# Attention output projection: one f32 product in column tiles, or three products of rounded parts in full tiles

## The chip, the cores and the metric

The kernel runs on one core of a Trainium2 chip. A core has five engines with queues of their own: TensorE (PE, matmuls), VectorE (DVE), ScalarE (ACT), GpSimd (POOL) and SyncE (SP, which here issues all DMA transfers). The metric is the device time of one execution in microseconds. Three runs of the kernel took 1322.6 us in the median, from 1322.46 to 1323.23.

## The reference, cut to what matters

Two independent halves are computed and set side by side: `a`, a long convolution of a state-space model (by Fourier transforms), and `b`, full attention with 16 heads of width 28 over 2048 positions. Here `x` is 1 x 2048 x 448, `wqkv` 448 x 1344 and `wo` 448 x 448, all in f32. The change lies in the last line of `b`, the product with `wo`.

```python
def _B_ref(x, wqkv, wo):
    B, S, D = x.shape
    H = 16; Dh = D // H
    qkv = (lambda x, *d: x.transpose(*d))((x @ wqkv).reshape(B, S, 3, H, Dh), 2, 0, 3, 1, 4)
    q, k, v = qkv[0], qkv[1], qkv[2]
    scale = Dh ** -0.5
    scores = jnp.einsum("bhqd,bhkd->bhqk", q, k) * scale
    p = _softmax(scores, axis=-1)
    o = jnp.einsum("bhqk,bhkd->bhqd", p, v)
    return (lambda x, *d: x.transpose(*d))(o, 0, 2, 1, 3).reshape(B, S, D) @ wo
...
return jnp.concatenate([a, b], axis=-1)
```

## The kernel before, in words

**Stages.** Up to about 255 us the kernel projects `q`, `k` and `v` and makes the seeds of the convolution's kernel. Then comes the attention, a loop over 256 steps, 16 units of 16 steps. A unit `u` is a group of four heads (`g = u // 4`) and a block of 512 queries (`c = u % 4`); a step `kt` is a block of 128 keys. So the units 12 to 15 are the last group of heads. All of the convolution's work is threaded into these steps, and the work of one step is one list, `ORDER`: score matmuls `s0` to `s3` (`pss`, each followed by an exponential on ACT into `p`), matmuls for the next unit's row maxima `m0` to `m3` (`pm`, reduced by DVE), the product with `v` of the step before (`pv`, into `po`), and free places `f`, `k` and `v` for the rest.

**Who goes when.** In this loop every engine's queue keeps the order in which the program names the instructions (`KEPT["a"]` lists all five). Each queue is worked off strictly in that order; an instruction that waits holds up all that is behind it on its engine. All instructions are recorded through one helper, so that the profile gives line 75 for nearly all of them; groups are told apart by the names of their tiles. The places `f` are given away by `slot`: to `urgent` tasks first, then to `p_due` (the projections), `m_due` (matmuls of the convolution's kernel), `u_due` (transforms of `u`), and last to the spectra and the final transforms (`f_slot`).

**POOL's part.** For each of 56 blocks `b` of channels POOL raises the powers `e` (nine instructions, `e_power`: tiles `e`, `eu`, `sdb`; a multiplication, a second one and an addition for 256, 512 and 1024 elements a partition). `k_begin` queues them every 3.5 steps, three per step. PE multiplies them with `g` in `k_mm` (`pm<-e,g`) some four steps later; ACT evacuates into `ko` and `yk`. The blocks take up the loop to about 1010 us; then POOL has only parts of the spectra (`p<-pr,pr`, `ut`).

**The end of a unit.** `fin(u, s_)` runs when a unit's last `pv` is done. ACT copies `po` into `o`. Two slots later `sums` gets the softmax's sums by matmuls with `sel`, DVE inverts them, ACT spreads them (`rb`). Four slots after the end `scale` turns them by matmuls with `ident`, and DVE multiplies: `on = o * pw`. For the groups 0 to 2 `on` is stored to DRAM (`on_d`, 128 x 512). For the last group `load_og` has brought the three other groups' blocks for these queries into `og` (issued at step 12 of the unit), and four tasks `project(t)` are put into `p_due`, one per step; each makes 128 rows of the output. `load_wo` has placed `wo` in two tiles of four groups of 128 rows, with zeros where a head's 28 rows end.

**The product with `wo`.** A `project` contracts over four groups of 128 rows. `mm32` splits each 128 x 128 by 128 x 448 product into four matmuls whose outputs are 32 partitions each, in the four column tiles of PE. Operands are f32, and PE makes two instructions of each such matmul.

**The end of the kernel.** After the 256 steps the remaining slots run: the end of unit 15, its four projections, and the last final transforms (`zi<-`, `ot`), one between two projections.

**Rounded parts.** Elsewhere the kernel already uses another way: an operand is rounded to `F32R` (the high part), the rest is what is left after subtracting it, also as `F32R`, and three products (high x high, high x rest, rest x high) are added up in PSUM. The projections of `q`, `k` and `v` are made so (`qk_proj`, `v_proj`), in full tiles, one instruction for each matmul.

## Time and profile before

| | |
|---|---|
| median of three runs | 1322.6 us (1322.46 to 1323.23) |
| profiled execution | 1324.8 us, span 1323.0 us |
| PE busy | 1235.2 us, 93% |
| weight loads | 705.6 us, 53% |
| DVE busy | 989.7 us, 75% |
| ACT busy | 953.3 us, 72% |
| POOL busy | 839.9 us, 63% |
| DMA | 205.4 MB, 155 GB/s in the mean |
| granted TensorE clock, mean | 0.973 |

The profile is of one execution. The slices are 40 equal parts of the span, 33 us each, and give the busy share in tenths. A line of a stretch gives its two ends, then for each engine the busy time and the number of instructions, the granted clock, the DMA share and GB/s. A line of the order of time gives start, duration, engine, source line, operation, output and inputs, shape and count; brackets at its end give how long the engine was idle before it and who ended that. Matmuls overlap, so that the distance between starts says more about PE's pace than a duration.

### The profile page before, as it was taken

To read this page: it belongs to the slowest core of one execution; us is meant where nothing else is said; L and a number is where in the kernel's file an instruction comes from. 1 tells how busy PE (TensorE), PEld (TensorE's weight loads), DVE (VectorE), ACT (ScalarE), POOL (GpSimd) and SP (SyncE) were. 2 spreads that over 40 slices of the span, in tenths; PEclk is the share of its full clock that TensorE was granted. 3 is DMA by queue.
4 is the path that set the end of the run, shared out by engine and by line. 5 is a ranking of instruction groups with operands and counts; after the bars stand their busy time and mean duration, and the time that the engine had idled before them with its cause. 6 is when DMAs were issued, how large, how long until landed. Compare 5 with 4: busy or idle time off the path is not lost.

```text
span 1323.0 us, 33194 instructions
## 1 busy us (share of the span) xinstructions
PE 1235.2 (93%) x12625; PEld 705.6 (53%) x12625; DVE 989.7 (75%) x2138; ACT 953.3 (72%) x2068; POOL 839.9 (63%) x704
## 2 busy tenths in 40 slices
PE   6878886899999999999999999999998999898997
PEld 5657763455555555555555555555555545444433
DVE  5897786877778777778778988889887857757311
ACT  5876762488888888888888888888886656655553
POOL 3686682398887788887689999899992212211211
PEclk9979888899999999999999999999999999999999
DMA  6677669836765546478534134642325543824485
GB/s 204 204 263 257 218 210 286 230 69 139 183 146 133 128 137 172 130 182 215 165 99 93 55 85 94 149 96 56 97 56 146 189 154 132 276 91 165 148 221 137
DMA packets 200088, 205.36 MB, mean 155 GB/s; under 512 B 95992, under 2 KB 158520, under 8 KB 197880
## 3 DMA queue, kind: packets, MB, share of 16 engines
q1 hardware_dynamic: 199928, 203.23, 54.8%
q8 instruction: 100, 1.64, 0.5%
q14 instruction: 60, 0.49, 0.1%
HBM read 120.73 MB, written 82.18 MB: 153 GB/s over the span
## 4 chain that ended last, share of the span: by engine, by line
PE 69%; DVE 15%; POOL 5%; ACT 4%; issue 3%; DMA 2%; SPq 0%; ACTq 0%; POOLq 0%; DVEq 0%
PE pm L75 39%; PE po L75 15%; PE pss L75 15%; DVE mx L75 3%; DVE tri L75 2%; DVE p L75 2%; DVE pr L75 2%; DVE rl L75 1%; POOL e L75 1%; POOL qhat L75 1%; DVE qhat L75 1%; ACT tri L75 1%; DVE sg L75 1%; DVE px L75 1%; ACT p L75 1%
## 5 line engine op out<-in xcount | busy, mean ns | idle before, releaser
L75 ACT ACTIVATE p<-pss 128x512 f32<-128x512 f32 x1024 | 561.4, 610 | 120.8 <-PE pss L75 118.2
L75 PE MATMUL pss<-qhat,khat 128*128 128x512 f32 x1024 | 402.8, 399 | 2.3 <-ACT p L75 2.3
L75 DVE TENSOR_REDUCE mx<-pm 128x1 f32<-128x512 f32 x500 | 321.5, 684 | 101.8 <-PE pm L75 100.2
L75 PE MATMUL pm<-khat,qhat 128*128 128x512 f32 x749 | 327.1, 440 | 14.4 <-DVE mx L75 6.9
L75 POOL TENSOR_TENSOR e<-e,sdb 128x256 f32<-128x256 f32 x168 | 202.2, 1203 | 118.0 <-ACT e L75 108.8
L75 PE MATMUL po<-p,v 128*32 128x512 f32 x2048 | 270.1, 596 | 0.0
L75 POOL TENSOR_TENSOR e<-e,eu 128x256 f32<-128x256 f32 x168 | 248.4, 1479 | 13.2
L75 PEld LDWEIGHTS pm<-khat,qhat 128*128 128x128 f32 x749 | 141.6, 189 | 210.6 <-ACT p L75 43.6
L75 DVE CUSTOM_DVE_ANT_0 rl<-pm,rl 128x512 f32<-128x512 f32 x249 | 171.5, 689 | 59.9 <-ACT rl L75 56.0
L75 PEld LDWEIGHTS pss<-qhat,khat 128*128 128x128 f32 x1024 | 190.8, 189 | 47.8 <-issue 11.8
L75 POOL TENSOR_TENSOR eu<-e,sdb 128x256 f32<-128x256 f32 x168 | 202.3, 1204 | 0.0
L75 POOL TENSOR_TENSOR p<-pr,pr 64x448 f32<-64x448 f32 x32 | 40.9, 1279 | 197.5 <-DVE pr L75 186.5
L75 ACT ACTIVATE rl<-pm 128x512 f32<-128x512 f32 x249 | 150.9, 606 | 20.8 <-PE pm L75 20.7
L75 DVE TENSOR_TENSOR g<-g,zg 128x128 f32<-128x128 f32 x392 | 162.3, 414 | 3.4
L75 PE MATMUL pm<-xh,khat 112*128 112x512 f32 x256 | 92.9, 447 | 21.9 <-DVE hl L75 9.5
L75 PE MATMUL pm<-kdif,qhat 128*128 128x512 f32 x249 | 101.4, 407 | 2.4 <-DVE mx L75 1.3
L75 DVE TENSOR_TENSOR zg<-g,zg 128x128 f32<-128x128 f32 x224 | 88.0, 393 | 5.1
L75 PEld LDWEIGHTS pm<-e,g 128*32 128x32 f32 x3584 | 57.2, 109 | 43.7 <-issue 17.0
L75 PE MATMUL pm<-e,g 128*32 128x64 f32 x3584 | 73.1, 222 | 1.9 <-POOL e L75 1.9
L75 PEld LDWEIGHTS pm<-xh,khat 112*128 112x128 f32 x256 | 54.0, 216 | 37.8 <-DVE hl L75 10.9
L75 ACT ACTIVATE y<-pm 128x448 f32<-128x448 f32 x48 | 26.3, 549 | 66.1 <-issue 33.0
L75 PEld LDWEIGHTS po<-p,v 128*32 128x32 f32 x2048 | 55.8, 110 | 22.3 <-issue 17.9
(135 smaller groups left out, 1504.6 us busy)
## 6 DMA issues: line engine op xcount, KB each, us to landing
sdb<-sd SPq DMA_DIRECT2D x56, 336.0 KB
khat<-k SPq DMA_DIRECT2D x64, 256.0 KB
qhat<-q SPq DMA_DIRECT2D x64, 256.0 KB
sd<-sg SPq DMA_DIRECT2D x8, 1456.0 KB
k<-hl SPq DMA_DIRECT2D x16, 512.0 KB
q<-hl SPq DMA_DIRECT2D x16, 512.0 KB
mw<-in_mw SPq DMA_DIRECT2D x16, 512.0 KB
sd<-qhat SPq DMA_DIRECT2D x8, 896.0 KB
```

Of the source, the lines that this page charges most:

```text
L75: i = f(*args, **kw)
```

## The change

The product with `wo` is made from rounded parts. `scale` multiplies `o` in place and then splits it: ACT copies it, rounded, into the first half of a tile `op`, and POOL subtracts that copy from `o` into the second half (DVE in unit 15). The store to `on_d` carries both halves, and `load_og` brings both back, as two transfers. The weights are split in the same way, one of the four groups per step, once the convolution's blocks are done and their pool is closed (`wh_open`, `split_wo`). The tiles `og` and `wh` lie in a new pool, in the place that the closed one left. `project` makes three full-tile matmuls of 448 columns for each group of rows, 12 in all, where `mm32` made 16 in column tiles. The order of the other work on every engine is as before.

```diff
-    on_d = [dram.tile([G, 128, CQ], F32, name=f"on_{c}") for c in range(NQ)]
+    on_d = [dram.tile([G, 2, 128, CQ], F32, name=f"on_{c}") for c in range(NQ)]
...
-    og_u = {}
+    og_u, wh, w_due = {}, {}, collections.deque()
 
     def load_og(u):
-        og_u[u] = og = kq_p.tile([128, G - 1, CQ], F32, name="og")
-        nc.sync.dma_start(og, on_d[u % NQ][:G - 1].rearrange("g p q -> p g q"))
+        og_u[u] = og = wh["p"].tile([128, G - 1, 2, CQ], F32R, name="og")
+        for i in range(2):
+            nc.sync.dma_start(og[:, :, i].bitcast(F32), on_d[u % NQ][:G - 1, i].rearrange("g p q -> p g q"))
+
+    def wh_open():
+
+        wh["p"] = pool(f1_st, "wh_p")
+        wh["w"] = wh["p"].tile([128, 2, G, D], F32R, name="wh")
+        w_due.extend(range(G))
+
+    def split(hi, lo, x_, e):
+        nc.scalar.activation(hi, x_, AF.Copy)
+        e.tensor_tensor(lo, x_, hi.bitcast(F32), ALU.subtract)
+
+    def split_wo(g2):
+        split(wh["w"][:, 0, g2], wh["w"][:, 1, g2], wo_t[g2 // 2][:, g2 % 2, :], nc.gpsimd)
...
-        on = kq_p.tile([128, CQ], F32, name="on", bufs=2)
+        op = kq_p.tile([128, 2, CQ], F32R, name="op")
...
-            nc.vector.tensor_tensor(on, o, pw, ALU.mult)
+            nc.vector.tensor_tensor(o, o, pw, ALU.mult)
+            split(op[:, 0], op[:, 1], o, nc.gpsimd if u < NU - 1 else nc.vector)
             if g < G - 1:
-                nc.sync.dma_start(on_d[c][g], on)
+                nc.sync.dma_start(on_d[c][g].rearrange("i p q -> p i q"), op.bitcast(F32))
...
+            n = 0
             for g2 in range(G):
-                mm32(pw[:, :D], og[:, g2, ts] if g2 < G - 1 else on[:, ts], wo_t[g2 // 2][:, g2 % 2, :],
-                     start=g2 == 0, stop=g2 == G - 1)
+                for i, k in ((0, 0), (0, 1), (1, 0)):
+                    nc.tensor.matmul(pw[:, :D], og[:, g2, i, ts] if g2 < G - 1 else op[:, i, ts], wh["w"][:, k, g2],
+                                     start=n == 0, stop=n == 3 * G - 1)
+                    n += 1
...
             f_ready["s", 1] = s + F1
+            wh_open()
...
+        if w_due and f_ready["s", 1] < s:
+            split_wo(w_due.popleft())
```

## The prediction

> **What bounds the kernel now.** I read the slices of the page first, then the stretches of 66 us, then the order of time around the places that the diff touches.

> ```profile
> PE   6878886899999999999999999999998999898997
> POOL 3686682398887788887689999899992212211211
> ```

> TensorE (PE) is busy in nearly every slice from the ninth on. POOL is at 9 from slice 21 to 30 and idle after that; so two stretches have to be priced apart, the middle, where POOL is full, and the end, where the projections run.

> ```profile
> 660.00:726.00 66.00, 64.08 (x777) 36.64 (x776) 55.22 (x132) 55.20 (x126) 57.78 (x46) 1.00 0.37 93
> 792.00:858.00 66.00, 65.81 (x765) 37.65 (x761) 58.12 (x140) 55.51 (x128) 61.60 (x48) 1.00 0.54 124
> 1188.00:1254.00 66.00, 59.64 (x652) 29.33 (x655) 40.46 (x66) 37.11 (x71) 17.52 (x12) 1.00 0.51 163
> ```

> The columns are PE, weight load, DVE, ACT, POOL, the clock, DMA. In 792 to 858 PE works 65.81 of 66 us: what makes PE wait there lengthens the kernel. POOL works 61.60, so it has 4.4 us in 66 to make up for any stop. In 660 to 726 PE is at 64.08, 1.7 us short of its neighbours; the reason is the key to this change:

> ```profile
> 666.26 0.85 POOL L75 MEMSET ua<- 128x896 f32 x1 [11.15 <-PE pm L75]
> 667.07 0.64 POOL L75 TENSOR_TENSOR e<-e,sdb 128x256 f32<-128x256 f32 x1
> 690.77 0.62 POOL L75 TENSOR_TENSOR e<-e,sdb 128x256 f32<-128x256 f32 x1
> 679.03 0.65 PE L75 MATMUL pm<-e,g 128*32 128x64 f32 x32 [0.62 <-POOL e L75]
> 690.86 0.65 PE L75 MATMUL pm<-e,g 128*32 128x64 f32 x32 [1.30 <-POOL e L75]
> ```

> POOL runs ahead of PE, reached a memset whose buffer PE still read, and stood 11.15 us. Its queue is in order: the powers `e` behind it came late, and PE waited 0.62 and 1.30 us for them. From 667.07 to 690.77 POOL makes two groups of nine `e` steps without a break, 11.85 us each.

> **The change, part by part.**

> *The projection on PE.* Sixteen projections of 16 matmuls in column tiles (32 instructions each, as f32 takes two) become 12 full-tile matmuls.

> ```profile
> 1249.61 0.59 PE L75 MATMUL pm<-zi,wb 128*32 128x224 f32 x8
> 1250.13 0.73 PE L75 MATMUL pss<-qhat,khat 128*128 128x512 f32 x2
> 1250.79 2.46 PE L75 MATMUL pm<-ua,og 128*32 128x448 f32 x24
> 1253.82 0.61 PE L75 MATMUL po<-p,v 128*32 128x512 f32 x4
> 1310.97 0.56 PE L75 MATMUL pm<-zi,wb 128*32 128x224 f32 x8
> 1311.35 2.44 PE L75 MATMUL pm<-ua,og 128*32 128x448 f32 x24
> 141.47 0.37 PE L75 MATMUL pm<-vh,xh 112*128 112x448 f32 x1
> 143.72 0.37 PE L75 MATMUL pm<-vh,xl 112*128 112x448 f32 x1
> ```

> Before: from the first projection matmul, 1250.79, to the next work, 1253.82: 3.03 us. After: the projection of `v` in the first phase has the very form (three products, rounded type, 448 columns); its twelve matmuls start between 141.47 and 143.72, 2.25 over eleven steps, 0.2045 us each, 2.46 us for twelve. Gain 0.57 us. Twelve projections stand inside the attention's steps, with a full-tile `pss` or tiled `po` on either side, so the number of changes between tiled and full work stays: 12 x 0.57 = 6.8. The last four stand among tiled work alone and get eight such changes: `zi` to `pss` takes 1250.13 - 1249.61 = 0.52, `zi` to tiled `og` 1311.35 - 1310.97 = 0.38, so 0.14 a change, 1.1 in all. Against that 3 x 0.55, and 0.25 for the first of them, which must wait for the new copy and subtraction of the last `o`; the end gains 0.8. Together 7.6 (bounds: 5, if loads of weights show or a step in the late part is held by ACT; 9.5, if no change costs).

> [...] The rows show 0.2045 in this kernel, with the weight loads, and I go by them.

> *The split of `o` in units 0 to 14.* An ACT copy and a POOL subtraction, both of 128x512, behind the DVE multiplication that wrote `on`. The multiplication itself stays. Prices:

> ```profile
> L75 ACT ACTIVATE rb<-r x16: 628/630/634, 321.7 to 1303.0; 128x512 f32<-128x512 f32 x16
> L75 POOL TENSOR_TENSOR vl<-tri,vh x4: 1182/1269/1424, 11.1 to 18.3; 112x448 fp32r<-112x448 f32 x4
> ```

> Copy 0.63, with two hand-overs (an estimate, 0.06 each) 0.75 from the end of the multiplication to the subtraction. Subtraction between 1.31 (an `e` step of this size, at 814.07 below) and 1.45 (`vl`, 1269 by 512/448): 1.4. The work is little; the place is what counts. In the built queue of the changed kernel each subtraction stands between the `e` steps that POOL did long before the multiplication. For unit 8:

> ```profile
> 814.07 1.31 POOL L75 TENSOR_TENSOR e<-e,eu 128x512 f32<-128x512 f32 x1
> 815.46 1.91 POOL L75 TENSOR_TENSOR e<-e,sdb 128x1024 f32<-128x1024 f32 x1
> 819.33 2.39 POOL L75 TENSOR_TENSOR e<-e,eu 128x1024 f32<-128x1024 f32 x1
> 824.42 0.68 DVE L75 TENSOR_TENSOR on<-o,pm 128x512 f32<-128x512 f32 x1
> 825.12 0.68 ACT L75 ACTIVATE yk<-pm 128x256 f32<-128x256 f32 x1 [0.97 <-PE pm L75]
> 830.53 0.65 PE L75 MATMUL pm<-e,g 128*32 128x64 f32 x32
> ```

> POOL is free at 815.4; the multiplication ends at 825.10, the copy is there at 825.85. POOL stands 10.5 us, subtracts until 827.25, and begins at that time what it began at 815.46: 11.8 late. The group that ended at 819.33 + 2.39 = 821.7 ends at 833.5; PE wants it at 830.53, and waits 3.0. Slack was 8.8. The first and the last such place, worked in the same way:

> ```profile
> 319.08 0.63 POOL L75 TENSOR_TENSOR e<-e,sdb 128x256 f32<-128x256 f32 x1 [3.70 <-ACT e L75]
> 325.27 0.69 DVE L75 TENSOR_TENSOR on<-o,pm 128x512 f32<-128x512 f32 x1
> 341.53 0.65 PE L75 MATMUL pm<-e,g 128*32 128x64 f32 x32
> 986.87 1.06 POOL L75 TENSOR_TENSOR e<-e,sdb 128x512 f32<-128x512 f32 x1
> 995.16 0.68 DVE L75 TENSOR_TENSOR on<-o,pm 128x512 f32<-128x512 f32 x1
> 1009.87 0.75 PE L75 MATMUL pm<-e,g 128*32 128x64 f32 x32
> ```

> Unit 0: 9.0 late against 10.5 of slack, nothing lost. Unit 11: 11.1 against 13.2, nothing. All twelve, late/slack: 9.0/10.5, 12.2/10.2, 10.8/8.8, 5.2/9.9, 10.5/9.6, 9.5/10.0, 4.6/1.8, 7.7/6.3, 11.8/8.8, 10.1/7.3, 5.2/7.0, 11.1/13.2. The excess: 1.9, 2.0, 0.9, 2.8, 1.4, 3.0, 2.8, sum 14.8; after units 7 and 8 POOL has no pause, so the next group is late too, 1.4 and 1.5: 17.7. Carried through in order, with what each PE wait gives back to POOL, it is 16.7; a little may be caught up, I take 16. Ends: 11 (subtraction 1.0, a fifth caught up) and 20 (copies held up by ACT's other work). Units 12 to 14 come when POOL has 10 to 18 us of work in 66, and cost nothing there.

> *The copies on ACT.* Unit 8's runs to 825.79 and pushes `yk` from 825.12 by 0.67; over the twelve places 0 to 0.67 each, 4.1 in all by the same working. PE needs `yk` and `ko` only slots later: between 0 and 4.1 (6, if each push goes on to the exponentials), I take 1.5.

> *The weights' split* (four copies, four subtractions, one per step) lies in the steps around 1040, where copies of 0.55 each (0.63 by 448/512) push ACT's `rl`, on which DVE's maxima wait: 0 to 2.2. Unit 14's copy stands in front of two exponentials:

> ```profile
> 1242.54 0.69 DVE L75 TENSOR_TENSOR on<-o,pm 128x512 f32<-128x512 f32 x1 [1.93 <-PE pm L75]
> 1242.94 1.08 ACT L75 ACTIVATE p<-pss 128x512 f32<-128x512 f32 x2 [0.25 <-PE pss L75]
> ```

> The multiplication ends at 1243.23, the copy at 1243.92, so they begin 1.0 later; ACT then has PE's next projection to catch up in. For both I take 1.0 (0 to 3.2). The subtractions lie in POOL's pauses of the late part.

> *Queues.*

> ```profile
> 1284.24 0.59 SPq L75 DMA_DIRECT2D og<-on  x1
> 1304.58 2.44 PE L75 MATMUL pm<-ua,og 128*32 128x448 f32 x24
> DMA packets 200088, 205.36 MB, mean 155 GB/s; under 512 B 95992, under 2 KB 158520, under 8 KB 197880
> ```

> The store of `on` has the same place on SP and waits 2.2 us longer, for POOL; `yk` stores and `sdb` loads behind it are for later steps. Stores double to 512 KB; `og` comes as two loads of 768 KB, four steps ahead of need. I cost all at nothing: the last load is issued at 1284.24 and first read at 1304.58, and its doubled 1.57 MB take 10 us at the mean rate. Without those 20 us of cover it would cost up to that.

> *Sum:* +16 +1.5 +1.0 -7.6 = +10.9. The profiled run took 1324.8 (span 1323.0 and 1.8 around it), so 1335.7 on its scale; it lies 2.2 above the median of the runs, 1322.6, and by that the forecast is 1333.5.

> **The rivals.** *PE catches up (faster).* Place: the steps right behind each wait. While PE stands, ACT and DVE empty their queues, so PE later waits less for them.

> ```profile
> PEld pm L75 <- DVE mx L75: 78.1, 196, 3.0
> ```

> 78.1 us of such waits of the weight loads speak for it. From the point where less than 5 of the 16 us stay, the 7.6 win: with 1 us left the time is 1322.6 + 1 + 2.5 - 7.6 = 1318.5. Against it: 660 to 726 lost 1.7 of the 1.9 us waited, so next to nothing came back.

> *The clock falls too (slower still).*

> ```profile
> 1009.18 0.51 PE L75 MATMUL pm<-khat,qhat 128*128 128x512 f32 x1 [2.60 <-DVE mx L75]
> 1010.30:1013.70 3.40, 3.40 (x41) 1.35 (x30) 0.23 (x2) 0.48 (x2) 0.00 (x0) 0.50 0.02 5
> ```

> A wait of 2.60 us was followed by 3.4 us at half clock, 1.7 us lost; the wait of 1.30 above was not. Three or four of the new waits are 2.6 to 3.0: 4 x 1.7 = 6.8 on top, 1340. [...]

> *The projection is not faster.* If full tiles of 128 rows in the late part ran at 0.25 us, 12 take 3.0: 1341. Against it: the rows of `v`, 112 rows, at full clock.

> **How the numbers follow.** Forecast 0.62 (its own range 1326 to 1339); catching up 0.14; clock 0.15; projection 0.09. A difference under 0.2% (2.6 us) is what a measurement of this kernel cannot tell from none. Faster: 0.11 of the 0.14. Same: the other 0.03 and 0.02 of the forecast's low end. Slower: 0.84. The range from 1322 to 1342 leaves out most of the catching up and the top of the two slow rivals, some 0.2.

> **What would show it.** POOL standing 4 to 11 us in front of each `op` until ACT's copy, twelve times up to 1010; PE waits of 1 to 3 us for POOL `e`, some 12 to 20 us in all instead of two waits; unit 11's multiplication some 16 us later than 995; twelve projection matmuls in 2.46 us, and the stretch from unit 12's first projection to the end some 6 us shorter. It is wrong if POOL stands and PE's waits for `e` stay short, or if the copies on ACT cost PE more than POOL does.

## The result, and the profile after

The changed kernel took 1340.2 us in the median of four runs (1335.2 to 1341.4), the kernel before 1322.9 beside it (1322.5 to 1324.8). The ratio is 1.012, with an interval from 1.010 to 1.014: slower. The forecast was 1333.5, so the sign was right and the size 6.7 us short: +17.3 against a forecast of +10.9. 1340.2 lies just above the forecast's own range (1326 to 1339) and inside the whole one (1322 to 1342).

The profiled execution took 1335.2 us (span 1333.4), the fastest of the four. First the slices of the changed kernel's page, then two of the stretches of 66 us (columns as before: PE, weight load, DVE, ACT, POOL, clock, DMA):

```profile
PE   7879975899999999999999999899998999898998
POOL 3686671496969797959698987989994312212311
```

```profile
660.00:726.00 66.00, 61.49 (x748) 35.19 (x747) 52.87 (x126) 53.34 (x122) 58.57 (x48) 1.00 0.40 97
792.00:858.00 66.00, 60.49 (x737) 34.30 (x733) 52.34 (x125) 51.97 (x118) 58.22 (x47) 1.00 0.47 110
```

POOL's slices, which were 6 to 9 in the middle, now swing between 5 and 9. In 792 to 858 PE works 60.49 us where it worked 65.81: 5.3 us less in this stretch alone, with POOL at 58 of 66. Both stand, each for a part of the time. The waits show for whom (who waits, tile, for whom and for what: us in all, times, longest):

```profile
POOL op L75 <- ACT op L75: 98.0, 14, 13.7
...
PE pm L75 <- POOL e L75: 15.9, 10, 2.6
```

POOL stands 98 us in front of the new subtraction, waiting for ACT's copy; 80 us of that lie in front of the subtractions of units 0 to 11 (11.3, 10.8, 9.2, 6.3, 9.2, 7.9, 3.3, 4.6, 5.9, 4.1, 1.2, 6.4). PE's waits for `e`, two before, are ten by this view; an eleventh, of 1.27 us at 784.56, is put down to DVE there. One case from end to end, unit 8 of the changed kernel in order of time:

```profile
824.31 1.30 POOL L75 TENSOR_TENSOR e<-e,eu 128x512 f32<-128x512 f32 x1
830.09 0.68 DVE L75 TENSOR_TENSOR o<-o,pm 128x512 f32<-128x512 f32 x1
830.81 0.63 ACT L75 ACTIVATE op<-o 128x512 fp32r<-128x512 f32 x1 [0.99 <-DVE o L75]
831.52 1.29 POOL L75 TENSOR_TENSOR op<-o,op 128x512 fp32r<-128x512 f32 x1 [5.90 <-ACT op L75]
839.01 0.65 PE L75 MATMUL pm<-e,g 128*32 128x64 f32 x32 [2.52 <-POOL e L75]
```

POOL is done with `e` at 825.6 and stands 5.90 us until DVE has multiplied and ACT has copied; then it subtracts for 1.29 us. PE pays 6 us later, with 2.52 us.

To place the loss, I set the start of each product with `v` (`po<-p,v`, the same 2048 matmuls in every kernel) in a profile against the same matmul's start in the kernel before. The table gives how far the loop begins later (+) or earlier, what is then lost or won in each part, and the difference of the spans. It has all profiles of the study, one execution each, so that the experiments can be read from it; the names are those used below.

| profile | loop begins | units 0 to 11 | unit 12 | units 13 to 15 | after the loop | span |
|---|---|---|---|---|---|---|
| changed, first | -4.0 | +16.7 | +5.0 | -6.3 | -1.0 | +10.3 |
| changed, again | -1.4 | +18.3 | +4.7 | -4.9 | -1.1 | +15.7 |
| changed, third | -1.3 | +18.2 | +4.9 | -7.7 | -1.1 | +13.0 |
| wait and work | -0.6 | +11.6 | +1.7 | 0.0 | 0.0 | +12.7 |
| work only | +0.7 | +1.0 | -0.1 | +1.2 | 0.0 | +2.8 |
| later | +1.2 | +1.8 | +2.1 | -7.6 | -1.1 | -3.5 |
| DVE | +1.9 | +15.9 | +3.5 | -6.3 | -1.1 | +13.9 |
| split late | +0.8 | -0.4 | +3.2 | -4.4 | -1.0 | -1.8 |
| weights moved | -2.1 | +2.3 | +0.3 | -7.7 | -1.1 | -8.3 |
| copy moved | -3.1 | +2.2 | +1.8 | -7.6 | +0.4 | -6.2 |

The first column is not the change: the change adds no work ahead of the loop, and the column scatters from -4.0 to +1.9. So the first profile of the changed kernel flatters it by 4.0 us, and what the change costs is read from the loop on. The last columns hold some scatter of the granted clock too. In unit 13 of the kernel before it fell to half for 3.41 us, at 1146.8. In the four profiles of the changed kernel and its variants with -6.3, -4.9 or -4.4 it fell there as well, for 6.83 us in "changed, again"; in the four with -7.6 or -7.7 it did not. "Work only" has +1.2 because it stayed at half for 6.83 us there, and "copy moved" has +0.4 after the loop with a fall at 1298.

### The profile page after: what moved, and what is told of

Its sections match the earlier page's. It is cut to its first block, busy times and chain, and to the rows that moved or that the text cites. A ratio compares the mean times of both kernels' runs of the same rounds, so it can differ in the third digit from the quotient of the medians.

```text
span 1333.4 us, 32597 instructions
## 1 busy us (share of the span) xinstructions
PE 1227.5 (92%) x12305; PEld 719.3 (54%) x12305; DVE 992.2 (74%) x2139; ACT 963.8 (72%) x2088; POOL 862.1 (65%) x723
## 4 chain that ended last, share of the span: by engine, by line
PE 58%; DVE 17%; POOL 11%; ACT 5%; issue 4%; DMA 3%; SPq 1%; POOLq 0%; ACTq 0%; DVEq 0%
PE pm L75 33%; PE po L75 13%; PE pss L75 12%; POOL e L75 6%; DVE mx L75 3%; POOL eu L75 2%; DVE rl L75 2%; DVE p L75 2%; DVE tri L75 2%; DVE pr L75 1%; ACT p L75 1%; DMA qhat<-q 1%; DVE sg L75 1%; ACT tri L75 1%; SPq L75 1%
## 5 line engine op out<-in xcount | busy, mean ns | idle before, releaser
L75 ACT ACTIVATE p<-pss 128x512 f32<-128x512 f32 x1024 | 560.9, 610 | 126.4 <-PE pss L75 124.1
L75 DVE TENSOR_REDUCE mx<-pm 128x1 f32<-128x512 f32 x500 | 321.4, 684 | 117.4 <-PE pm L75 116.0
L75 PE MATMUL pss<-qhat,khat 128*128 128x512 f32 x1024 | 403.3, 400 | 2.4 <-ACT p L75 2.3
L75 PE MATMUL pm<-khat,qhat 128*128 128x512 f32 x749 | 327.5, 440 | 16.7 <-DVE mx L75 8.5
L75 PE MATMUL po<-p,v 128*32 128x512 f32 x2048 | 270.9, 598 | 0.0
L75 POOL TENSOR_TENSOR e<-e,eu 128x256 f32<-128x256 f32 x168 | 247.8, 1475 | 13.2
L75 PEld LDWEIGHTS pm<-khat,qhat 128*128 128x128 f32 x749 | 141.7, 189 | 212.4 <-ACT p L75 42.8
L75 POOL TENSOR_TENSOR e<-e,sdb 128x256 f32<-128x256 f32 x168 | 202.2, 1203 | 60.5 <-ACT e L75 52.1
L75 DVE CUSTOM_DVE_ANT_0 rl<-pm,rl 128x512 f32<-128x512 f32 x249 | 171.5, 689 | 61.6 <-ACT rl L75 56.6
L75 PEld LDWEIGHTS pss<-qhat,khat 128*128 128x128 f32 x1024 | 190.8, 188 | 48.3 <-issue 11.8
L75 POOL TENSOR_TENSOR eu<-e,sdb 128x256 f32<-128x256 f32 x168 | 202.3, 1204 | 0.0
L75 ACT ACTIVATE rl<-pm 128x512 f32<-128x512 f32 x249 | 150.9, 606 | 20.6 <-PE pm L75 16.1
L75 DVE TENSOR_TENSOR g<-g,zg 128x128 f32<-128x128 f32 x392 | 162.1, 414 | 3.4
L75 POOL TENSOR_TENSOR p<-pr,pr 64x448 f32<-64x448 f32 x32 | 41.1, 1286 | 149.7 <-DVE pr L75 148.4
L75 PE MATMUL pm<-xh,khat 112*128 112x512 f32 x256 | 90.7, 437 | 22.3 <-DVE hl L75 10.5
L75 PE MATMUL pm<-kdif,qhat 128*128 128x512 f32 x249 | 101.5, 408 | 2.8 <-DVE mx L75 1.3
L75 DVE TENSOR_TENSOR zg<-g,zg 128x128 f32<-128x128 f32 x224 | 88.0, 393 | 5.0
L75 PEld LDWEIGHTS pm<-e,g 128*32 128x32 f32 x3584 | 57.5, 110 | 60.1 <-POOL e L75 24.6
L75 PE MATMUL pm<-e,g 128*32 128x64 f32 x3584 | 73.5, 222 | 17.2 <-POOL e L75 15.9
L75 POOL TENSOR_TENSOR op<-o,op 128x512 fp32r<-128x512 f32 x15 | 19.4, 1294 | 108.0 <-ACT op L75 98.0
L75 PEld LDWEIGHTS pm<-xh,khat 112*128 112x128 f32 x256 | 51.9, 208 | 38.5 <-DVE hl L75 13.2
L75 ACT ACTIVATE ub<-pm 128x224 f32<-128x224 f32 (+1 forms) x96 | 38.8, 450 | 39.6 <-PE pm L75 38.2
```

The costliest lines, as they stand in the source:

```text
L75: i = f(*args, **kw)
```

## Experiments

My theory was that the subtraction costs by its place in POOL's queue, not by its work. The rivals: that the work itself is too much for a POOL that is busy 61.6 of 66 us; that the copies on ACT or the split of the weights carry the loss; and, for the size, that the clock falls.

**Wait and work, and work only.** Two edits of the kernel before, told apart by the comments below, with nothing else of the change. The first gives POOL, at the end of each of the units 0 to 11, a 128x512 subtraction that reads `on`. The second gives it the same subtraction from a tile that is always ready. Its result `z` is used by nothing in either.

```diff
+    z = kq_p.tile([128, CQ], F32, name="z512")
+    nc.gpsimd.memset(z, 0.0)
...
             nc.vector.tensor_tensor(on, o, pw, ALU.mult)
+            if g < G - 1:
+                nc.gpsimd.tensor_tensor(z, on, z, ALU.subtract)   # first
+                nc.gpsimd.tensor_tensor(z, z, z, ALU.subtract)    # second, in its place
```

> The kernel before, and in the places of the first twelve subtractions one POOL subtraction of 128x512 that reads `on`; its result is used by nothing. No copy on ACT, no change of the projection. Theory (POOL stands in its queue until the multiplication is done, and the powers behind it come late): the lateness of each place is that of the prediction less the copy, 0.7 us; worked through in order, PE waits 11 us in units 1 to 9, so 1322.9 + 11 = 1334, and up to 3 more if a wait halves the clock. Rival A (it is the 1.3 us of work on a full POOL): the same as with a subtraction that waits for nothing. Rival B (the loss came from the copies on ACT): 1323.

> The same as the run before it, but the subtraction reads a tile that nobody else writes, so that it waits for nothing. Theory: 12 x 1.3 us on POOL are taken out of its lead and its pauses, PE does not wait for more than before, 1323 (within 1). Rival A (POOL is full, its work is the loss): 1334 as with the waiting one. Rival B (copies on ACT): 1323.

Measured: 1338.1 us with the wait (1337.6 to 1339.3), ratio to the kernel before 1.011 (1.008 to 1.014); 1324.7 without it, 1.001 (0.999 to 1.002). The same place in both, unit 8; the wait in the first, and the waits of that kernel behind it:

```profile
824.04 1.29 POOL L75 TENSOR_TENSOR e<-e,eu 128x512 f32<-128x512 f32 x1
830.56 1.30 POOL L75 TENSOR_TENSOR z<-on,z 128x512 f32<-128x512 f32 x1 [5.22 <-DVE on L75]
```

```profile
POOL z L75 <- DVE on L75: 72.8, 12, 10.7
...
PE pm L75 <- POOL e L75: 9.8, 8, 1.9
```

Work only:

```profile
816.97 1.31 POOL L75 TENSOR_TENSOR e<-e,eu 128x512 f32<-128x512 f32 x1
818.23 1.04 POOL L75 TENSOR_TENSOR z<-z 128x512 f32<-128x512 f32 x1
819.23 1.92 POOL L75 TENSOR_TENSOR e<-e,sdb 128x1024 f32<-128x1024 f32 x1
```

The work, 12 x 1.04 us (a little less than the 1.30 of the first edit), shows no cost that the runs can tell from none. One dependence on DVE makes a loss of 11.6 us in units 0 to 11, with neither copies nor weights in the kernel. Of these, 10.0 are new waits for `e` (the eight above and one of 2.10 that the view puts down to DVE, less the 1.9 us of the kernel before), and the clock fell once behind them, for 3.41 us at 838.9. The 1338.1 is some 4 us over the 1334 that was expected; up to 3 had been set aside for the clock, and the 1.7 us of unit 12 were not in it. The loss is less than in the changed kernel, as expected for a POOL that waits for DVE alone, without ACT's copy behind it. The place carries the cost; POOL's load does not.

**Later.** The changed kernel, with POOL's subtraction and the store queued six steps after the end of the unit, when the copy is long there. ACT's copy keeps its place.

```diff
...
-            split(op[:, 0], op[:, 1], o, nc.gpsimd if u < NU - 1 else nc.vector)
             if g < G - 1:
-                nc.sync.dma_start(on_d[c][g].rearrange("i p q -> p i q"), op.bitcast(F32))
+                nc.scalar.activation(op[:, 0], o, AF.Copy)
+                def rest():
+                    nc.gpsimd.tensor_tensor(op[:, 1], o, op[:, 0].bitcast(F32), ALU.subtract)
+                    nc.sync.dma_start(on_d[c][g].rearrange("i p q -> p i q"), op.bitcast(F32))
+                o_due.append((s_ + 6, rest))
             else:
+                split(op[:, 0], op[:, 1], o, nc.gpsimd if u < NU - 1 else nc.vector)
...
+        if o_due and o_due[0][0] <= s:
+            o_due.popleft()[1]()
...
```

> The changed kernel with one thing moved: in units 0 to 11 POOL's subtraction and the store behind it are queued at the start of the step six after the unit's end, some four steps later; the copy on ACT stays where it was. Same instructions, same engines. Theory: POOL's lead of up to 11.3 us is under three steps, so it finds the copy done and stands nowhere; the 16.7 us of units 1 to 10 go, the gain of the projections (7.4 from unit 13 on) stays, and so do some 3 of the 5 us in unit 12 (the weights' copies and the clock): 1340.2 - 16.7 - 2 = 1321, between 1316 and 1324. Rival B (the copies on ACT cost): 1335 or more, since they are all there.

Measured: 1318.9 us (1314.8 to 1321.8), ratio 0.995 (0.994 to 0.997): faster than both kernels, as expected (1321, between 1316 and 1324). Its waits:

```profile
PE pm L75 <- POOL e L75: 1.9, 2, 1.3
...
POOL op L75 <- ACT op L75: 16.5, 2, 12.4
```

The 16.5 us are those of units 13 and 14, where PE has no work of `e` left to wait for. PE waits for `e` twice, 1.9 us, as before the change. Of the 16.7 us in units 0 to 11 there remain 1.8, which hold the price of the copies on ACT and of the subtractions' work. The late part is 8.7 us shorter; some 7.3 of these are the projections' (the first profile has -6.3 and -1.0 with the clock falling in unit 13 as it did before), and the rest came at the end of unit 13, where the clock did not fall in this execution. The rival that the copies on ACT carry the loss asked for 1335 or more and falls. So the projection was worth having, and one place in a queue had turned it into a loss.

**DVE.** The other way off POOL's queue: the subtraction on DVE in all units.

```diff
-            split(op[:, 0], op[:, 1], o, nc.gpsimd if u < NU - 1 else nc.vector)
+            split(op[:, 0], op[:, 1], o, nc.vector)
```

> The changed kernel with the subtraction on DVE in all units, right behind the multiplication. Theory: POOL has no new work and no wait, so the 16.7 us go; but DVE now stands 0.75 us for ACT's copy and works 0.69, 1.4 us at each unit's end, 12 times in a stretch where it is busy 58 of 66 us: between 0 and 17 us of it reach PE, I take 6: 1340 - 16.7 - 2 + 6 = 1327. If DVE hides it, 1321. Rival A (POOL's work): below 1327 as well. Rival B (the copies on ACT): 1335 or more.

Measured: 1334.7 us (1333.8 to 1338.8; the profile is of the slowest run), ratio 1.009 (1.005 to 1.012). This was a miss. It comes out near rival B's figure, but "later", with all the copies, has ruled that rival out. I had counted the hand-over and 0.69 us per unit, and most of it as hidden. The subtractions of this kernel (16; shortest, median and longest, ns), then unit 8's with POOL's work beside it, then PE's waits for DVE's maxima in this kernel, and the same line of the kernel before:

```profile
L75 DVE TENSOR_TENSOR op<-o,op x16: 691/977/2428, 328.6 to 1321.3; 128x512 fp32r<-128x512 f32 x16
```

```profile
838.69 1.30 POOL L75 TENSOR_TENSOR e<-e,eu 128x512 f32<-128x512 f32 x1
838.73 1.81 DVE L75 TENSOR_TENSOR op<-o,op 128x512 fp32r<-128x512 f32 x1 [0.70 <-ACT op L75]
```

```profile
PE pm L75 <- DVE mx L75: 21.5, 29, 2.6
```

```profile
PE pm L75 <- DVE mx L75: 10.4, 18, 2.6
```

POOL has its lead back: PE waits for `e` twice, 1.9 us, as before the change. But DVE stands 0.70 us for the copy, and then its subtraction takes up to 2.43 us and not 0.69. Unit 8's began 0.04 us after a step of POOL's powers and ended 0.55 after that step's end. So it is with all twelve that began while POOL worked on `e`: each ended 0.55 to 0.58 us after the end of a step that was running when it began. The four of units 12 to 15, with POOL idle, took 0.69 us. PE's waits for the maxima go from 10.4 us to 21.5. So DVE, which feeds PE step by step in this kernel, paid for its short wait and its longer subtraction at once (11.1 us more of these waits), while POOL, which runs ahead, paid only where its lead was used up: of the 80 us that it stood in the changed kernel in front of the subtractions of units 0 to 11, 15.3 reached PE.

**Weights moved, and copy moved.** Two trials at what "later" leaves. The first takes the split of the weights out of step 14 of unit 12 (it goes to step 15), where it stood before ACT's `rl`. The second also defers ACT's copy of `o` to the fifth step after the end.

```diff
-        if w_due and f_ready["s", 1] < s:
+        if w_due and f_ready["s", 1] < s and kt != 14:
...
-                nc.scalar.activation(op[:, 0], o, AF.Copy)
+                o_due.append((s_ + 5, lambda: nc.scalar.activation(op[:, 0], o, AF.Copy)))
```

> The kernel with the later subtraction, and the last of the four splits of the weights one step later (step 15 of unit 12 in place of step 14). In step 14 PE stood 2.43 us, the clock then fell to half for 3.4 us, and unit 12 lost 2.5 us in all. Theory: the copy of 0.58 us in front of the exponentials of step 14 is the cause (it delays ACT's `rl`, and in the built queue a matmul of that step waits for DVE's `mh` in place of ACT's `rl`); with the copy moved PE waits under 1 us there, and 2 to 2.5 us go: 1318.9 - 2.3 = 1316.6. Rival (any place costs the same, or the fall of the clock comes by itself): 1319.

> As the run before it, and in units 0 to 11 the copy on ACT is moved too, to the start of the step before the subtraction. In the run with the later subtraction units 0 to 11 still lost 1.9 us. Theory: that is ACT standing for the multiplication and then pushing `yk` and `ko`; where the copy finds its input done, only its work of 0.63 is left, and 1 of the 1.9 us goes: 1315.6. Rival (it is ACT's work that counts): no change, 1316.6, or worse by up to 12 x 0.2 if exponentials are pushed.

Measured: 1320.1 us (1316.1 to 1321.3), ratio 0.995 (0.994 to 0.997), and 1319.0 (1316.7 to 1320.9), ratio 0.995 (0.994 to 0.997). Neither is better than "later", 0.995, so the rivals of both expectations hold and the gains do not come. The place in "later", and the same place with the weights moved:

```profile
1056.15 0.75 PE L75 MATMUL pm<-khat,qhat 128*128 128x512 f32 x1 [2.42 <-DVE mh L75]
```

```profile
1050.28 0.50 PE L75 MATMUL pm<-khat,qhat 128*128 128x512 f32 x1 [0.77 <-ACT rl L75]
...
1052.03 1.44 PE L75 MATMUL pm<-p,mw 128*32 128x224 f32 x16 [1.02 <-DVE mh L75]
```

One wait of 2.42 us became two of 0.77 and 1.02, which saves 0.6. But the clock fell to half for 3.41 us right there all the same, at 1052.4. The table's +0.3 for unit 12 is better than "later" mostly because the clock, in that one execution, did not fall at 1010; "copy moved", with the same place for the weights and that fall, has +1.8. Deferring the copy changed nothing in units 0 to 11 (+2.2 against +2.3).

**Split late.** The changed kernel, but `o` of units 0 to 11 is stored unsplit, loaded as one transfer, and the three blocks are split after that, in the steps 13 to 15 of units 12 to 15. Nothing of the split is left in units 0 to 11.

```diff
...
+    def split_og(u, g2):
+        og = og_u[u]
+        split(og[:, g2, 0], og[:, g2, 1], og[:, g2, 1].bitcast(F32), nc.gpsimd)
...
-                nc.sync.dma_start(on_d[c][g].rearrange("i p q -> p i q"), op.bitcast(F32))
+                nc.sync.dma_start(on_d[c][g], o)
...
-        if kt == 12 and u // NQ == G - 1:
+        if kt == 9 and u // NQ == G - 1:
             load_og(u)
+        if kt > 12 and u // NQ == G - 1:
+            split_og(u, kt - 13)
```

> The changed kernel, but `o` of units 0 to 11 is stored unsplit as before the change, and split after it is loaded: in the steps 13 to 15 of units 12 to 15 one group each, copy on ACT, subtraction on POOL; the load is issued at step 9. Theory: nothing new stands in POOL's or ACT's queue up to 1010 us, so units 0 to 11 take what they took before (the 16.7 us and the copies' 1.9 go); the projections' 7.4 us stay; the twelve late copies of 0.63 lie in steps in which ACT has 37 to 40 us of work in 66, and cost 0 to 7.6, I take 3; unit 12 keeps its 2.5: 1323.8 + 2.5 + 3 - 7.5 = 1321.8. Rival (the split costs the same wherever it stands): 1335 or more.

Measured: 1322.7 us (1320.8 to 1324.5), ratio 0.998 (0.997 to 0.999): faster than before by about the 2 us that were expected, but not by as much as "later". Units 0 to 11 cost nothing (-0.4), and the late part gives less: -4.4 in units 13 to 15, not -7.6. In unit 13 ACT's first copy stands in front of `rl`, POOL's subtraction takes 1.54 us beside DVE's work, and PE waits 1.80 us for DVE's maxima:

```profile
1131.63 0.63 ACT L75 ACTIVATE og<-og 128x512 fp32r<-128x512 f32 x1
1132.15 0.60 ACT L75 ACTIVATE rl<-pm 128x512 f32<-128x512 f32 x1
1132.59 1.54 POOL L75 TENSOR_TENSOR og<-og 128x512 fp32r<-128x512 f32 x1
1133.75 0.96 PE L75 MATMUL pm<-p,mw 128*32 128x224 f32 x16 [1.80 <-DVE mx L75]
```

The same matmul waits 0.38 us in "later":

```profile
1133.87 0.96 PE L75 MATMUL pm<-p,mw 128*32 128x224 f32 x16 [0.38 <-issue]
```

Which of the two, copy or subtraction, makes this wait was not separated. The rest of the difference is the clock, which in this execution fell in unit 13, as in the kernel before, and in that of "later" did not.

**The changed kernel, again and a third time.** Its median is 5 us above its first profile.

> The changed kernel once more, for a second execution to look into: its median lies 5 us above the one that was profiled. Theory: what differs between its executions lies ahead of the loop (the profiled one came to the loop 4.0 us earlier than the kernel before did); from unit 1 to unit 10 TensorE again falls back by 16 to 17 us, and the projections again give 7 to 8 back, so that a time of 1340 has a loop that begins 4 to 5 us later than in the first profile. Rival: the waits for POOL of 2.5 us and more are followed by the half clock in some executions (1.7 us each) and not in others; then units 1 to 10 lose 18 to 23 us and the loop begins as it did.

> The same kernel a third time, with the same two expectations: units 1 to 10 lose 16 to 17 us whatever the time (the difference lies ahead of the loop), or 18 to 23 us with granted clocks of 0.5 behind the waits of 2.5 us (the clock is the difference).

Measured: 1340.5 and 1337.8 us, one run each. Both expectations were right in part, as the table shows. Of the 5.4 us between the spans of the first and second profile (1333.4 and 1338.7), 2.6 lie ahead of the loop. The waits for `e` are the same to 0.1 us, but units 0 to 11 lose 18.3 and 18.2 in place of 16.7, and this difference is the clock. The wait for unit 6's late `e`, in the first and in the second profile, with the stretches of one clock window (3.413 us) around it:

```profile
719.32 0.65 PE L75 MATMUL pm<-e,g 128*32 128x64 f32 x32 [2.56 <-POOL e L75]
```

```profile
714.92:718.33 3.41, 1.83 (x8) 1.12 (x6) 2.21 (x5) 2.92 (x7) 3.33 (x3) 1.00 0.69 170
718.33:721.74 3.41, 2.42 (x44) 1.45 (x45) 0.44 (x1) 0.56 (x3) 3.25 (x5) 1.00 0.08 28
721.74:725.15 3.41, 3.41 (x49) 1.92 (x49) 3.31 (x10) 2.86 (x8) 3.25 (x4) 1.00 0.25 77
```

```profile
721.90 0.97 PE L75 MATMUL pm<-e,g 128*32 128x64 f32 x28 [2.57 <-POOL e L75]
```

```profile
718.50:721.91 3.41, 0.84 (x5) 0.36 (x3) 1.22 (x3) 2.08 (x5) 3.33 (x3) 1.00 0.57 144
721.91:725.32 3.41, 3.41 (x42) 1.65 (x43) 0.00 (x0) 0.41 (x2) 3.25 (x5) 0.50 0.00 0
```

The wait is as long in both. In the first it is cut in two by a border between windows, so that PE is busy 1.83 and 2.42 of 3.41 us in the two, and the clock stays at 1.00. In the second it lies in one window, PE is busy 0.84 us in it, and the next one runs at 0.50.

## Why the prediction was right, and where it was not

*The subtraction's place in POOL's queue: right, in mechanism and size.* POOL stood in front of each `op`, 1.2 to 11.3 us (4 to 11 foretold), and PE stood 17.2 us in front of the products of `e`, in eleven waits of which ten name POOL (12 to 20 foretold). The kernel before has 1.9 of these 17.2 too, so 15.3 are new, where 16 stood in the sum. With the copies, the prediction had 17.5 us; units 0 to 11 lost 16.7, and in the other two profiles 18.2 and 18.3, of which some 1.5 are the clock. Single places came out otherwise than worked: in unit 8 POOL stood 5.90 us and not 10.5, since it came there 10 us later than before (825.6 against 815.4) and the multiplication only 5.7; PE's wait was 2.52 against 3.0. From the end of the multiplication to the subtraction it is 0.75 us there, as costed; the two hand-overs in it, 0.06 each by an estimate, took 0.04 and 0.08. Unit 11's multiplication ended 12.7 us later than before, in a loop that began 4.0 earlier: 16.7. "Wait and work" shows the cause by adding it alone, "later" by taking it away.

*The copies on ACT: 1.5 taken, 1.8 to 2.3 measured*, together with the subtractions' work ("later", "weights moved"). That the copies alone make it was not separated; "work only", without copies, has +1.0 in the same units.

*The projection: right.* Twelve matmuls inside the attention, from the first to the next work, and one projection of the end, both of the changed kernel:

```profile
1258.14 1.99 PE L75 MATMUL pm<-wh,og 128*128 128x448 f32 x9
1259.97 0.77 PE L75 MATMUL pm<-wh,op 128*128 128x448 f32 x3
1260.67 0.64 PE L75 MATMUL po<-p,v 128*32 128x512 f32 x4
...
1319.39 2.09 PE L75 MATMUL pm<-wh,og 128*128 128x448 f32 x9
...
1322.02 0.59 PE L75 MATMUL pm<-zi,wb 128*32 128x224 f32 x8
```

1260.67 - 1258.14 is 2.53 us, where 2.46 was foretold and 3.03 stood before. At the end it is 1322.02 - 1319.39 = 2.63, with the changes between tiled and full work. The whole of it gave 7.3 us in the first profile (6.3 and 1.0), 7.6 foretold. The rival that full tiles run at 0.25 us here falls.

*The split of the weights and unit 14's copy: wrong, and the largest miss.* I took 1.0 us, with an end at 3.2; unit 12 lost 4.7 to 5.0. Two things were missing. The first is not the weights at all. At the start of unit 12 POOL, now late, still worked on `e` when DVE came to its part of the spectra. DVE and POOL of the kernel before, and the same two and PE after:

```profile
1004.99 2.62 POOL L75 TENSOR_TENSOR p<-pr,pr 64x448 f32<-64x448 f32 x2 [8.34 <-DVE pr L75]
1005.41 2.68 DVE L75 TENSOR_TENSOR p<-pr,pr 64x448 f32<-64x448 f32 x2
```

```profile
1017.99 2.37 POOL L75 TENSOR_TENSOR e<-e,eu 128x1024 f32<-128x1024 f32 x1
1018.17 4.14 DVE L75 TENSOR_TENSOR p<-pr,pr 64x448 f32<-64x448 f32 x2
1020.44 2.86 POOL L75 TENSOR_TENSOR p<-pr,pr 64x448 f32<-64x448 f32 x2
...
1023.39 0.80 PE L75 MATMUL pm<-khat,qhat 128*128 128x512 f32 x1 [4.05 <-DVE mx L75]
```

DVE's two multiplications take 4.14 us in place of 2.68. PE, which waited 2.60 here before, waits 4.05, and the clock is half for 6.83 us in place of 3.41. Together that is 2.4 us. "Wait and work" has it too (+1.7 in unit 12, without any weights); "later", where POOL is on time, has DVE's 2.68 us back and loses nothing here:

```profile
1008.49 2.68 DVE L75 TENSOR_TENSOR p<-pr,pr 64x448 f32<-64x448 f32 x2
```

The second is in steps 13 and 14, some 2.5 us, and is the weights'. PE before, and ACT and PE after:

```profile
1051.78 0.50 PE L75 MATMUL pm<-khat,qhat 128*128 128x512 f32 x1 [0.80 <-ACT rl L75]
...
1053.26 0.96 PE L75 MATMUL pm<-p,mw 128*32 128x224 f32 x16 [0.76 <-DVE mh L75]
```

```profile
1066.33 0.58 ACT L75 ACTIVATE wh<-ua 128x448 fp32r<-128x448 f32 x1
1066.79 0.60 ACT L75 ACTIVATE rl<-pm 128x512 f32<-128x512 f32 x1
...
1068.63 0.50 PE L75 MATMUL pm<-khat,qhat 128*128 128x512 f32 x1 [2.43 <-DVE mh L75]
```

With a copy in front of ACT's `rl` PE waited 2.43 us where it had waited 0.80 and 0.76, and the clock fell behind it, for 3.41 us at 1069.9. "Later" still has it (2.42, above), and with that copy moved it goes back to two short waits, but the clock falls all the same: these steps lost 2.4 us in "later" and still 2.0 with the weights moved. Unit 14's copy lies in unit 15, which gains 2.0 us, as unit 14 does with 2.1: no loss shows there. The fall of the clock behind a wait of 2.60 us, at 1010.30 in the kernel before, was in the text for a rival on the twelve waits on POOL, and was not applied to this term.

*The rivals.* That PE catches up falls: the 15.3 us of new waits, with the copies, cost 16.7. That the clock falls behind the waits for `e`, four times for 6.8 us on top, was wrong in its place: it fell at none of them in the first profile and at one in each of the two others. The median, 1340.2, equals that rival's figure, but by other places: in the profile of 1340.5 us the loop and its end lose 17.1 where 10.9 were foretold; 3.7 of the difference are unit 12, 1.6 the late part, mostly a clock that stayed at half for a second window at 1169, and 0.8 the units 0 to 11 with their one fall. All the same the clock is a good part of the miss. In that profile six windows of the loop run at half where the kernel before has two; at half of PE's busy time in them this is some 5.5 us more (an estimate), and one of the six stands behind a wait for `e`. In the two other profiles four windows run at half, some 2.6 us more. The sum had no term for that.

*Queues at nothing: right so far as the runs go.* No wait of the changed kernel's PE names a transfer of `og`, and "later", which has the doubled stores, lost no more than 1.8 us in units 0 to 11 for everything that is new there.

## What to carry to other kernels

Here POOL works through its queue in order and runs ahead of its reader, and one instruction that depends on late work cost the lead, not its own time: units 0 to 11 lost 11.6 us with the wait ("wait and work") and 1.0 with the work alone. Where an engine does so, work out for each place how late it makes the queue and how much lead there is, and queue it some steps later if the result is not needed yet ("later", 1.8 us in those units). Moving that instruction to an engine without lead was no cure; 0.69 us of work on DVE became 0.1 to 2.6 us a unit on the path of PE, 1.3 in the mean. And the shift of several microseconds in POOL changed which instructions ran side by side (DVE's two multiplications of unit 12, 2.68 us before and 4.14 after) and where the clock fell (3.41 us at half there before, 6.83 after), so that a term costed at about nothing wants its neighbours looked up at the new times.

## What the runs showed of the hardware

**DVE's work on two operands, beside POOL's.** In "DVE" the subtraction of two operands took 0.69 us with POOL idle and up to 2.43 with POOL at work, and it ended 0.55 to 0.58 us after a POOL step in all twelve cases of the second kind. Of the two multiplications of unit 12 the first took 2.67 us in the changed kernel, where a step of `e` ran until 0.47 us before its end, and 1.21 in "later", where POOL was past `e` at the same place. The other way round shows once in "later": a POOL subtraction that began 0.41 us before the end of DVE's multiplications took 1.53 us, where the other fourteen of that kernel took 1.28 to 1.30. What holds the one back beside the other, the traces do not show.
